# A fused gated linear attention and MLP kernel: first unit loaded and scanned in halves, three whole-weight tiles made split ones, a new order of the work, other idle fill-ups

## The chip, the cores and the metric

One core of a Trainium2 chip runs the kernel. Its engines are TensorE (PE, matrix products), VectorE (DVE), ScalarE (ACT), GpSimd (POOL) and SyncE (SP, which here only issues DMAs). The metric is the time of one execution on the chip in microseconds, the median of several runs.

## The reference

Gated linear attention over B=4 batches, H=8 heads, S=768 tokens and head size D=48, then an MLP on the heads put side by side (3072 tokens of 384 values, inner size 2048):

```python
f = 1.0 / (1.0 + np.exp(-f_logit))
for t in range(S):
    state = f[:, :, t, :, None] * state + np.einsum('bhd,bhe->bhde', k[:, :, t], v[:, :, t])
    y[:, :, t] = np.einsum('bhd,bhde->bhe', q[:, :, t], state)
x = y.transpose(0, 2, 1, 3).reshape(B * S, H * D)
h = x @ w_in                                   # 384 -> 2048
g = h * np.clip(h + 3.0, 0.0, 6.0) / 6.0
out = g @ w_out                                # 2048 -> 384
```

## The kernel before

**Units.** The attention goes in 24 units, each 128 tokens (a chunk, in two halves of 64) of one batch with all heads. A step of unit *i* is written `step.i`:

- `load`, `loadq`, `loadv`: DMAs of the gate logits, of q and k together, and of v, issued by SP.
- `gate` (L321, ACT): the sigmoid. `back` (L327, DVE): a scan backwards through the chunk, giving for each token the product of the gates behind it. `rend` (L343 and L344, DVE): the chunk's whole product, and one over it. `kmul` (L340, DVE or POOL): k times that scan. `fwd` (L347, DVE): the scan forwards. `qmul` (L353): q times it. `decay` (L356): the old state times the chunk's product.
- `tk` (L411, PE): transposes of k, copied out by `ktok` (L418, ACT). `kv` (L430, PE): the chunk's new state, added by `carry0` and `carry1`. `att` (L392, PE): scores of queries with keys, and `mask` (L399, DVE), which copies them out under the causal triangle. `qs` (L461) and `av` (L478, PE): queries with states, and scores with values, into one bank.
- `xh`, `xl`: the result x as two float16 parts, high and low. Where the order holds an `xs` (L501, PE), PE subtracts the high part in its bank and ACT writes `xl`; else DVE does. `hole`: a DMA that packs the rows.

**Weights.** They come as float64 bits in 16 tiles *f*: `ld` (DMA), then `z`, `cy`, `mid`, `dif`, `top` (integer operations on ACT and DVE that round the bits to float32: `whole`), then `high` and `low` (float16 parts: `weight`; `lowi` and `lowo` are the halves of `low` for `w_in` and `w_out`, in tiles 0 to 7).

**The MLP.** Tokens go in groups of up to 512, numbered so that the step of group *g* and tile *f* has index 16 *g* + *f*. `mm1` (L536): nine float16 products of 512 columns. `relu` (ACT), `g` (L550, DVE): the activation. `gh` (L555, ACT) and `gl` (L565, DVE or POOL): its float16 parts. `mm2` (L582): nine float16 products into three banks that stay open for the group. In the first group the tiles 0 to 4 are done in half groups, `mm1a`, `mm1b` (L603), `ga`, `gb` and `mm2a`, `mm2b` (L621), whose second products are float32 with `whole`. Its tiles 5, 6 and 7 have whole groups, but `mm2x` (L593): three float32 products of 512 columns with `whole`, without `gh` and `gl`.

**The order.** A table of words, `ORDER`, holds every step. The code walks it and emits each step's instructions, and a chain of dependencies then keeps each engine's instructions in just that order. The number behind a PE step is the PSUM bank. A table `ON_POOL` names the steps that go to GpSimd instead of DVE. So the order of the words sets what each queue waits for. Buffers are rings: gates and scans have three (unit 3 uses unit 0's), q/k and v four each.

**Idle products.** At the start the table holds words `warm.N`: float32 products of a zero tile `blank` into a bank that nobody reads, N times 128 columns:

```python
if op == "warm":
    for at in range(0, i, 4):
        n = min(i - at, 4)
        nc.tensor.matmul(
            idle[:, :n * 128].rearrange("p (a n) -> p a n", n=128), blank,
            blank.unsqueeze(1).broadcast_to([128, n, 128]), start=True, stop=True,
        )
```

Of the kernel before, what the change touches and what calls it, by code (L numbers as in the profile page):

```python
# [48 lines left out]
kmul.1 decay.4 kmul.6 lowi.5 kmul.7 decay.7 lowi.7 kmul.8 gl.9 decay.8 gl.11 qmul.8 gl.12 lowo.0 low.15 lowo.3 gl.19  # L49
decay.9 qmul.10 gl.25 kmul.12 gl.26 qmul.12 gl.27 gl.28 gl.29 gl.32 gl.33 decay.14 kmul.14 kmul.15 qmul.15 gl.37 gl.38  # L50
gl.39 gl.40 kmul.16 decay.15 gl.44 qmul.16 gl.45 gl.47 decay.17 kmul.18 gl.51 gl.52 gl.53 gl.54 gl.55 kmul.19 gl.57
decay.19 decay.20 kmul.20 qmul.20 kmul.21 gl.60 qmul.21 decay.22 gl.62 kmul.23 qmul.23 gl.70 gl.72 gl.74 gl.73 gl.75
gl.76 gl.77
# [3 lines left out]
carry0.0 load.2 qmul.0 warm.1 att.0.0 loadq.1 ld.0 rend.1 qs.0.2 mask.0 gate.2 warm.1 av.0 xh.0 kmul.1 tk.1.4 ktok.1  # L57
carry1.0 fwd.1 qmul.1 warm.3 att.1.0 xs.0 loadv.1 back.2 mask.1 rend.2 cy.0 load.3 kv.1.2 z.0 mid.0 loadq.2 gate.3
back.3 ld.1 carry0.1 warm.1 qs.1.0 dif.0 kmul.2 top.0 fwd.2 xl.0 carry1.1 loadq.3 av.1 hole.0 tk.2.4 rend.3 xh.1 xs.1
xl.1 z.1 qmul.2 warm.3 att.2.2 kmul.3 cy.1 mid.1 fwd.3 ktok.2 loadv.2 high.0 warm.4 kv.2.0 carry0.2 tk.3.4 ktok.3  # L60
mask.2 load.4 gate.4 qs.2.0 hole.1 av.2 xh.2 carry1.2 lowi.0 mm1a.0.4 relua.0 dif.1 qmul.3 top.1 high.1 ga.0 loadv.3
xs.2 att.3.2 mask.3 kv.3.0 ld.2 carry0.3 carry1.3 lowi.1 xl.2 loadq.4 warm.1 qs.3.2 av.3 xh.3 mm1a.1.4 cy.2 xs.3 xl.3
relua.1 z.2 back.4 kmul.4 rend.4 fwd.4 ga.1 decay.4 mm2a.0 qmul.4 load.5 gate.5 tk.4.1 mm2a.1 ktok.4 loadv.4 ld.3 cy.3
z.3 hole.2 mid.2 dif.2 top.2 att.4.2 kv.4.2 hole.3 mm1b.0.0 high.2 back.5 mid.3 relub.0 loadq.5 mm1b.1.1 relub.1
lowi.2 gb.0 dif.3 kmul.5 rend.5 gb.1 mm1a.2.4 mm1b.2.0 top.3 mm2b.0 mm2b.1 fwd.5 tk.5.1 relua.2 relub.2 gb.2 qmul.5
ld.4 z.4 cy.4 mid.4 mm2b.2 high.3 ktok.5 lowi.3 ga.2 mm1b.3.0 load.6 gate.6 loadq.6 dif.4 back.6 top.4 load.7 mm1a.3.4
ld.5 relub.3 mm2a.2 relua.3 ga.3 high.4 gb.3 cy.5 z.5 mask.4 mm2a.3 lowi.4 mm1a.4.1 relua.4 rend.6 ld.6 mm1b.4.4
relub.4 loadv.6 gate.7 loadq.7 mm2b.3 carry0.4 kmul.6 fwd.6 mid.5 ga.4 dif.5 z.6 qmul.6 top.5 cy.6 tk.6.1 ktok.6
mm2a.4 back.7 ld.7 decay.5 high.5 qs.4.2 decay.6 att.5.0 gb.4 av.4 kv.6.0 carry1.4 lowi.5 mm1.5.4 mask.5 mm2b.4
carry0.6 xh.4 z.7 xl.4 mid.6 dif.6 kmul.7 carry1.6 loadv.5 kv.5.2 ld.8 relu.5 g.5 mm2x.5 cy.7 top.6 high.6 cy.8 rend.7  # L70
tk.7.0 mid.7 dif.7 load.8 lowi.6 carry0.5 top.7 mm1.6.4 ktok.7 qs.5.2 fwd.7 qmul.7 high.7 loadv.7 relu.6 g.6 z.8
# [887 lines left out]
```

## Time and profile before

| | |
|---|---|
| time, three runs | 467.69, 466.12, 467.33 us, median 467.33 |
| the profiled execution | 468.3 us, its span 466.6 us, mean granted PE clock 0.993 |
| PE busy | 459.2 us (98%) |
| DVE busy | 300.1 us (64%) |
| ACT busy | 205.1 us (44%) |
| POOL busy | 79.3 us (17%) |
| DMA | 43.09 MB, mean 92 GB/s |

The span is what the profiler saw of the program; the execution's own time holds 1.7 us around it. Engines overlap, so the shares don't add up. Rows of a timeline hold a group of neighbouring instructions of one form: start, length in us, engine, line, operation, out<-in with shapes, and how many; a bracket holds the idle time ahead of it and what ended that. "xN" behind a PE row counts instructions as the profiler does: a float32 product is two of them, a float16 product one.

### The profile page before, as it was taken

The page shows a single profiled execution, that of the slowest core. Times are in us where ns is not written, and L with a number is a line of the kernel's source. Part 1 is how long each engine was busy: PE and PEld are TensorE (multiplying, and loading weights), DVE is VectorE, ACT ScalarE, POOL GpSimd, SP SyncE. Part 2 cuts the span into 40 slices and gives each one's busy share as a digit, 9 for nine tenths or more (in the row PEclk, how much of TensorE's full clock was granted, in tenths as well). Part 3 has the DMA queues.
Part 4 walks back from the last instruction along what each step waited for, and adds up shares of the span by engine and source line. Part 5 has one row for each costly group of instructions (what it writes and reads, how often), then busy time and mean ns, then how long its engine had stood idle before and what let it go on. Part 6 is the DMA issues. An engine that isn't in the chain of part 4 may idle for free.

```text
span 466.6 us, 11487 instructions
## 1 busy us (share of the span) xinstructions
PE 459.2 (98%) x4963; PEld 247.5 (53%) x4963; DVE 300.1 (64%) x508; ACT 205.1 (44%) x344; POOL 79.3 (17%) x85
## 2 busy tenths in 40 slices
...
PEclk9799999999999999999999999999999999999999
...
GB/s 301 188 249 353 249 181 249 198 84 0 135 108 1 51 206 0 153 46 0 87 31 91 42 94 1 196 90 76 4 80 0 1 0 6 24 45 3 0 1 68
DMA packets 25396, 43.09 MB, mean 92 GB/s; under 512 B 2560, under 2 KB 17152, under 8 KB 25344
## 3 DMA queue, kind: packets, MB, share of 16 engines
...
q8 instruction: 39, 0.64, 0.6%
...
## 4 chain that ended last, share of the span: by engine, by line
PE 97%; DVE 1%; ACT 1%; issue 1%; DVEq 0%
PE o L582 35%; PE pair L536 26%; PE single L536 13%; PE pair L461 3%; PE o L621 3%; PE pair L478 3%; PE pair L392 3%; PE pair L430 2%; PE idle L804 2%; PE o L593 2%; PE pair L636 1%; PE single L636 1%; PE single L603 1%; PE pair L603 1%; PE pair L411 1%; PE single L411 1%
## 5 line engine op out<-in xcount | busy, mean ns | idle before, releaser
L582 PE MATMUL o<-gg,weight 128*128 128x512 f16 x744 | 170.2, 379 | 0.0
L536 PEld LDWEIGHTS <-weight 128*128 128x128 f16 x819 | 78.7, 98 | 93.6 <-issue 0.8
L536 PE MATMUL pair<-xts,weight 128*128 128x512 f16 x549 | 125.9, 379 | 0.0
L582 PEld LDWEIGHTS <-weight 128*128 128x128 f16 x744 | 72.0, 98 | 82.4 <-issue 0.7
L555 ACT ACTIVATE gg<-tg 128x512 f16<-128x512 f32 x88 | 54.5, 627 | 62.5 <-DVE tg L550 56.1
L550 DVE SCALAR_TENSOR_TENSOR tg<-tg,pair 128x512 f32<-128x512 f32 x61 | 41.3, 682 | 62.7 <-ACT tg L546 62.6
L546 ACT ACTIVATE tg<-pair,half 128x512 f32<-128x512 f32 x61 | 41.5, 683 | 66.6 <-PE pair L536 64.8
L565 POOL TENSOR_TENSOR gg<-tg,gg 128x512 f16<-128x512 f32 x33 | 40.1, 1225 | 167.1 <-ACT gg L555 148.1
L536 PE MATMUL single<-xts,weight 128*128 128x512 f16 x270 | 63.3, 379 | 0.0
L550 DVE SCALAR_TENSOR_TENSOR tg<-tg,single 128x512 f32<-128x512 f32 x30 | 20.5, 683 | 33.2 <-ACT tg L546 33.2
L546 ACT ACTIVATE tg<-single,half 128x512 f32<-128x512 f32 x30 | 20.6, 686 | 45.0 <-PE single L536 43.3
L347 DVE TENSOR_TENSOR_SCAN suffix<-gates,rend 112x516 f32<-112x516 f32 x24 | 30.6, 1276 | 4.3 <-POOL qkf L340 3.7
L327 DVE TENSOR_TENSOR_SCAN suffix<-gates,unit 112x516 f32<-112x516 f32 x24 | 29.9, 1248 | 5.1 <-ACT gates L321 5.0
L565 DVE TENSOR_TENSOR gg<-tg,gg 128x512 f16<-128x512 f32 x39 | 27.0, 702 | 8.4 <-ACT gg L555 8.2
L497 ACT ACTIVATE xts<-pair 112x512 f16<-112x512 f32 x24 | 14.3, 595 | 30.2 <-PE pair L478 17.8
L340 POOL TENSOR_TENSOR qkf<-qkf,suffix 112x512 f32<-112x512 f32 x13 | 17.0, 1309 | 47.1 <-DVE suffix L327 43.4
L399 DVE TENSOR_TENSOR a<-pair,causal 128x512 f32<-128x512 f32 x24 | 16.4, 684 | 13.0 <-PE pair L392 10.2
L510 DVE SCALAR_TENSOR_TENSOR xts<-pair,xts 112x512 f16<-112x512 f32 x20 | 13.6, 682 | 8.5 <-ACT xts L497 8.4
L321 ACT ACTIVATE gates<-gates 112x512 f32<-112x512 f32 x24 | 14.9, 623 | 5.2 <-DMA gates<-fg 5.2
L430 PE MATMUL pair<-v,ktok 64*48 64x48 f32 (+1 forms) x768 | 15.8, 214 | 1.3 <-issue 1.3
L478 PE MATMUL pair<-a,v 64*48 64x64 f32 (+1 forms) x768 | 16.2, 222 | 0.6 <-DVE a L399 0.2
L392 PE MATMUL pair<-qkf 48*64 48x64 f32 x768 | 16.4, 224 | 0.2 <-ACT state L450 0.2
...
## 6 DMA issues: line engine op xcount, KB each, us to landing
...
xts<-xts SPq DMA_DIRECT2D x48, 24.0 KB, 1.9
...
```

The lines of the kernel that those rows point to most:

```text
L327: nc.vector.tensor_tensor_scan(flat(sf)[:, ::-1], gt[:, 1:][:, ::-1], flat(unit)[:, ::-1], 0.0, op0=ALU.mult, op1=ALU.add,)
L340: engine("kmul", i).tensor_tensor(parts_of(t, 1), parts_of(t, 1), split(sf[:, :, 1:C + 1]), op=ALU.mult)
L347: nc.vector.tensor_tensor_scan(flat(sf), gt[:, :NP * (C + 1)], flat(rend), 0.0, op0=ALU.mult, op1=ALU.add,)
L392: nc.tensor.matmul(d["at"][HC * odd:HC * (odd + 1), e, 2 * n + c], t[rs, 1, n, c, odd], t[rs, 0, n, c, odd], start=True, stop=True,)
L430: nc.tensor.matmul(d["kv"][r:r + m, odd, c, n], d["ktok"][rs, 2 * n + part, r:r + m], heads_of(vt[rs], part, n, e)[:, :D], start=(odd, e) ...
L478: nc.tensor.matmul(d["y"][to:to + m, odd, n, cs], heads_of(vt[rs], c, n, e)[:, :m], d["a"][rs, 2 * n + c, e], start=False, stop=True, skip ...
L536: nc.tensor.matmul(h, win[:, f, a, k * 128:(k + 1) * 128], g["xt"][:, k, :g["n"] // C, b], start=i == 0, stop=i == 3 * KT - 1,)
L546: nc.scalar.activation(d["t"], d["h"], AF.Relu, bias=half, scale=RISE)
L550: nc.vector.scalar_tensor_tensor(d["t"], d["t"], TOP, d["h"], op0=ALU.min, op1=ALU.mult)
L555: nc.scalar.activation(d["gg"][:, 0], d["t"], AF.Copy)
L565: engine("gl", int(g["name"]) * NF + f).tensor_tensor(d["gg"][:, 1], d["t"], d["gg"][:, 0], op=ALU.subtract)
L582: nc.tensor.matmul(g["o"][m], wout[:, f, a, m * 128:(m + 1) * 128], g[f]["gg"][:, b], start=f == 0 and i == 0, stop=f == NF - 1 and i == 2 ...
```

## The change

*The first unit.* Its gate logits come in two DMAs, `load.0` and `loadh.0`, and sigmoid and first scan are two each, `gate.0`, `gateh.0` and `back.0`, `backh.0`. k and q of this unit come apart, `loadk.0` ahead of `loadv.0` and `loadq.0`. All go by SP, as before.

*The start.* A dummy sigmoid that stood among the constants is now a word of the table (`table.0`), and one constant is set by DVE instead of POOL. A `brief.84` word makes 84 bfloat16 products of 64x64 columns on a zero tile; with `warm.8` behind them, two products of 512 columns, they stand where `warm.16`, four of them, stood. The other fill-ups ahead of the first model product were 4, 1, 1, 3, 1, 3 and 4 (x128 columns) and are 2, 7, 3, 1 and 3; the 1 behind it stays.

*Whole-weight tiles.* `mm2x` of tiles 5, 6 and 7 go; these tiles have `gh`, `gl` and the nine-product `mm2`, and their `lowo` stand earlier. `xs.4` and `xs.5` are new, so `xl.4` and `xl.5` go from DVE to ACT.

*The order and the engines.* The table is another one throughout. `ON_POOL` changes too: of the first group and the units beside it, `kmul.1`, `gl.9`, `gl.11`, `gl.12` and `lowo.3` go to DVE, and `lowi.0`, `lowi.6`, `decay.5`, `decay.6` and `gl.8` to GpSimd. Two output steps change their kind (`outv.4` to `outs.4`, `outs.6` to `outv.6`), and two output pieces of the fourth group are no longer written in halves.

```diff
-HALVED = [("3", 0), ("3", 1), ("4", 0), ("4", 1), ("4", 2)]
+HALVED = [("4", 0), ("4", 1), ("4", 2)]
 ...
 ORDER = """
-load.0 gate.0 back.0 loadq.0 loadv.0 rend.0 kmul.0 load.1 fwd.0 gate.1 back.1 warm.16 tk.0.3 ktok.0 warm.4 kv.0.0
 ...
+load.0 loadh.0 loadk.0 load.1 loadv.0 loadq.0 table.0 gate.0 loadq.1 gateh.0 gate.1 back.0 backh.0 kmul.0 brief.84 warm.8
+tk.0.2 rend.0 fwd.0 back.1 qmul.0 ktok.0 warm.2 kv.0.2 carry0.0 carry1.0 load.2 kmul.1 warm.7 tk.1.4 ktok.1 rend.1
 ...
+    small = const.tile([128, 128], BF16, name="small")
+    nc.vector.memset(small, 0.0)
     blank = const.tile([128, 128], F32, name="blank")
     nc.vector.memset(blank, 0.0)
     half = const.tile([128, 1], F32, name="half")
-    nc.gpsimd.memset(half, 2.0 ** (GBITS - HBITS - 1))
+    nc.vector.memset(half, 2.0 ** (GBITS - HBITS - 1))
     table = const.tile([128, 1], F32, name="table")
-    nc.scalar.activation(table, half, AF.Sigmoid)
 ...
+    def halved(sf, gt, rows):
+        fu = unit.rearrange("r p c -> r (p c)")
+        fs = sf.rearrange("r p c -> r (p c)")
+        n = NP // 2 * (C + 1)
+        cuts = 0, n + 1, FW
+        ops = {}
+        for p, name in enumerate(("", "h")):
+            lo, hi = cuts[p:p + 2]
+            at, two = slice(p * n, (p + 1) * n), slice(p * NP // 2, (p + 1) * NP // 2)
+            def load(_=None, lo=lo, hi=hi):
+                nc.sync.dma_start(out=gates[0][:, lo:hi], in_=fg[0][:, lo:hi])
+            def gate(_=None, two=two):
+                nc.scalar.activation(rows[:, two], rows[:, two], AF.Sigmoid)
+            def back(_=None, at=at):
+                nc.vector.tensor_tensor_scan(
+                    fs[:, at][:, ::-1], gt[:, 1:][:, at][:, ::-1], fu[:, at][:, ::-1], 0.0, op0=ALU.mult, op1=ALU.add,
+                )
+            ops.update({"load" + name: load, "gate" + name: gate, "back" + name: back})
+        def loadk():
+            t = sb.tile([128, 2, NP, C], F32, tag="qkf", name="qkf0")
+            nc.sync.dma_start(out=t[:, 1], in_=qk[0][:, 1])
 ...
+        def loadq():
+            nc.sync.dma_start(out=ops["tile"][:, 0], in_=qk[0][:, 0])
+        def first():
+            nc.scalar.activation(table, half, AF.Sigmoid)
 ...
+        if i == 0:
+            ops.update(halved(sf, gt, rows))
 ...
-        if op == "warm":
+        if op == "brief":
+            for _ in range(i):
+                nc.tensor.matmul(idle[:64, :64], small[:, :64], small[:, :64], start=True, stop=True)
+        elif op == "warm":
```

The order as the engines get it. TensorE from its first instruction to the first unit's `av`, before (`pair` and `single` are PSUM banks, `qkf` holds q and k, `a` the masked scores):

```order
L804 MATMUL idle<-blank 128x512 x4
L411 MATMUL pair_71<-ident,qkf_132 128x112 x4
L804 MATMUL idle<-blank 128x512
L430 MATMUL pair_70<-v_134,ktok_151 64x48
...
L804 MATMUL idle<-blank 128x128
L392 MATMUL pair_70<-qkf_132 64x64 x16
L461 MATMUL pair_71<-qkf_132,middle_101 64x64 x8
L804 MATMUL idle<-blank 128x128
L478 MATMUL pair_71<-a_212,v_134 64x64 x8
L478 MATMUL pair_71<-a_212,v_134 48x64 x8
L411 MATMUL single<-ident,qkf_198 128x112 x4
```

and in the changed kernel, where lines are shifted (L845 the small products, L849 the idle products, L453 `tk`, L472 `kv`, L434 `att`, L503 `qs`, L520 `av`):

```order
L845 LDWEIGHTS small
L845 MATMUL idle<-small 64x64
...
L849 MATMUL idle<-blank 128x512 x2
L453 MATMUL pair_71<-ident,qkf_132 128x112 x4
L849 MATMUL idle<-blank 128x256
L472 MATMUL pair_71<-v_135,ktok_242 64x48
...
L849 MATMUL idle<-blank 128x384
L453 MATMUL single<-ident,qkf_140 128x112 x4
L434 MATMUL pair_70<-qkf_132 64x64 x16
L503 MATMUL pair_71<-qkf_132,middle_102 64x64 x8
L849 MATMUL idle<-blank 128x384
L520 MATMUL pair_71<-a_300,v_135 64x64 x8
```

The second unit's `tk` (into `single`) has moved from behind the first unit's `av` to ahead of its `att`, and the small products, 168 instructions, stand at the head.

VectorE up to the mask of the third unit, `mask.2`. Before, from `mid.0` (L256) on:

```order
L256 TENSOR_SCALAR raw_200<-top_270 128x768
...
L343 TENSOR_SCALAR ends<-suffix_76 112x4
L344 RECIPROCAL rend<-ends 112x4
L353 TENSOR_TENSOR qkf_299<-qkf_299,suffix_80 112x512
L340 TENSOR_TENSOR qkf_321<-qkf_321,suffix_76 112x512
L256 TENSOR_SCALAR raw_303<-top_372 128x768
L347 SCALAR_TENSOR_TENSOR suffix_76<-gates_75,rend 112x516
L399 TENSOR_TENSOR a_413<-pair_71,causal 128x2x4x64
```

and in the changed kernel (L441 is the mask, L383 and L384 `rend`, L257 `mid`, L387 `fwd`):

```order
L367 SCALAR_TENSOR_TENSOR suffix_76<-gates_75,unit 112x516
L393 TENSOR_TENSOR qkf_417<-qkf_417,suffix_80 112x512
L380 TENSOR_TENSOR qkf_463<-qkf_463,suffix_76 112x512
L441 TENSOR_TENSOR a_499<-pair_71,causal 128x2x4x64
L383 TENSOR_SCALAR ends<-suffix_76 112x4
L384 RECIPROCAL rend<-ends 112x4
L257 TENSOR_SCALAR raw_495<-top_504 128x768
L387 SCALAR_TENSOR_TENSOR suffix_76<-gates_75,rend 112x516
```

`rend.3`, `mid.1` and `fwd.3` stood ahead of `mask.2` and now stand behind it. `kmul.1`, on GpSimd before, is now a step of DVE, the third behind `fwd.0`, and `back.0` is two scans of 258 columns.

More of the change, by code (lines that the diff above doesn't have):

```diff
@@ L48 @@
 ON_POOL = """
[L49 to L53, printed above, removed]
+lowi.0 decay.5 decay.4 kmul.6 decay.6 lowi.5 kmul.7 lowi.6 lowi.7 kmul.8 gl.8 decay.7 decay.8 qmul.8 low.15 gl.15
@@ L57 @@
[L57 to L71, printed above, removed]
@@ L72 @@
-decay.7 att.6.0 ld.9 lowi.7 gate.8 av.5 cy.9 z.9 mask.6 mm1.7.4 relu.7 mid.8 dif.8 top.8 mid.9 carry1.5 dif.9 high.8
-low.8 mm2x.6 mm1.8.0 g.7 loadq.8 ld.10 top.9 xh.5 cy.10 relu.8 high.9 back.8 rend.8 mm2x.7 ld.11 xl.5 g.8 att.7.2 z.10
-cy.11 qs.6.0 kv.7.2 mid.10 load.10 loadv.8 av.6 dif.10 low.9 top.10 z.11 mid.11 gh.8 mm1.9.4 ld.12 ld.14 xh.6 xl.6
-gl.8 mm2.8 dif.11 high.10 low.10 relu.9 g.9 cy.12 mm1.10.1 top.11 mask.7 kmul.8 carry0.7 gh.9 gl.9 hole.4 relu.10
-high.11 mm2.9 carry1.7 g.10 low.11 z.12 mid.12 ld.13 dif.12 top.12 cy.13 gh.10 gl.10 tk.8.1 ktok.8 mm1.11.0 z.13
@@ new lines @@
+tk.0.2 rend.0 fwd.0 back.1 qmul.0 ktok.0 warm.2 kv.0.2 carry0.0 carry1.0 load.2 kmul.1 warm.7 tk.1.4 ktok.1 rend.1
+fwd.1 att.0.0 mask.0 qs.0.2 warm.3 av.0 qmul.1 gate.2 back.2 att.1.0 mask.1 ld.0 z.0 load.3 xh.0 xs.0 cy.0 mid.0
+loadv.1 rend.2 dif.0 kv.1.2 carry0.1 carry1.1 warm.1 qs.1.0 av.1 xl.0 loadq.2 kmul.2 tk.2.4 gate.3 xh.1 ktok.2 top.0
+fwd.2 back.3 qmul.2 loadv.2 xs.1 kv.2.2 xl.1 high.0 carry0.2 loadq.3 warm.3 att.2.2 qs.2.0 kmul.3 tk.3.4 ld.1 z.1
+lowi.0 mask.2 load.4 hole.0 cy.1 rend.3 ktok.3 av.2 xh.2 gate.4 hole.1 mm1a.0.4 relua.0 xs.2 loadv.3 mid.1 fwd.3 dif.1
```

159 lines of the change are left out of this document (91 added, 68 removed).

## The prediction

> **What bounds the kernel now.** I read the page first, then a table of windows, then the first 30 us instruction by instruction.
>
> ```profile
> PE 459.2 (98%) x4963; PEld 247.5 (53%) x4963; DVE 300.1 (64%) x508; ACT 205.1 (44%) x344; POOL 79.3 (17%) x85
> PEclk9799999999999999999999999999999999999999
> q8 instruction: 39, 0.64, 0.6%
> PE 97%; DVE 1%; ACT 1%; issue 1%; DVEq 0%
> ```
>
> TensorE (PE) is busy for 98% of the span and carries 97% of the chain; its clock is below full speed only near the start. So time is won in two ways only: fewer columns for PE, or an earlier dense stage. Windows show who leads at the start (from 40 us on PE has no hole):
>
> ```profile
> 10.00:20.00 10.00, 8.17 (x222) 6.18 (x222) 9.66 (x15) 4.96 (x11) 0.45 (x1) 0.84 0.59 234
> 30.00:40.00 10.00, 9.87 (x169) 8.26 (x168) 9.83 (x18) 8.33 (x15) 0.51 (x1) 1.00 0.64 234
> 40.00:80.00 40.00, 40.00 (x553) 27.56 (x551) 37.49 (x71) 29.60 (x44) 6.44 (x6) 1.00 0.68 255
> 25.03:101.80 76.77, 76.46 (x1149) 50.85 (x1140) 68.78 (x122) 57.64 (x89) 12.99 (x13) 1.00 0.64 234
> 13.40:16.80 3.40, 1.93 (x74) 1.44 (x74) 3.33 (x7) 2.39 (x5) 0.00 (x0) 1.00 0.65 261
> 16.80:20.20 3.40, 3.31 (x66) 2.66 (x66) 3.40 (x6) 1.19 (x4) 0.00 (x0) 0.50 0.05 13
> 20.20:23.60 3.40, 3.40 (x40) 2.12 (x39) 1.37 (x4) 2.64 (x5) 0.00 (x0) 0.50 0.53 153
> ```
>
> After the window's length the columns are PE, weight loads, VectorE (DVE), ScalarE (ACT), GpSimd, then clock, DMA share and GB/s. DVE is full while the first units pass (9.66 of 10) and still 94% busy from 40 to 80 us, so it sets when PE can begin its dense stage, and may set its pace afterwards. The clock fell to half from 16.8 to 23.6 us.
>
> The DVE queue, by its timeline (start, duration):
>
> ```profile
> 4.13 1.23 DVE L327 TENSOR_TENSOR_SCAN suffix<-gates,unit 112x516 f32<-112x516 f32 x1 [2.32 <-ACT gates L321]
> 5.40 0.17 DVE L343 TENSOR_SCALAR ends<-suffix 112x4 f32<-112x4 f32 x1
> 5.77 0.66 DVE L340 TENSOR_TENSOR qkf<-qkf,suffix 112x512 f32<-112x512 f32 x1
> 6.46 1.23 DVE L347 TENSOR_TENSOR_SCAN suffix<-gates,rend 112x516 f32<-112x516 f32 x1
> 7.61 1.21 DVE L327 TENSOR_TENSOR_SCAN suffix<-gates,unit 112x516 f32<-112x516 f32 x1
> 10.89 0.69 DVE L399 TENSOR_TENSOR a<-pair,causal 128x512 f32<-128x512 f32 x1 [0.20 <-PE pair L392]
> 20.07 0.15 DVE L343 TENSOR_SCALAR ends<-suffix 112x4 f32<-112x4 f32 x1
> 20.34 0.66 DVE L353 TENSOR_TENSOR qkf<-qkf,suffix 112x512 f32<-112x512 f32 x1
> 23.61 0.36 DVE L256 TENSOR_SCALAR raw<-top 128x768 int16<-128x768 int16 x1 [2.00 <-ACT top L252]
> 23.89 1.23 DVE L347 TENSOR_TENSOR_SCAN suffix<-gates,rend 112x516 f32<-112x516 f32 x1
> 25.03 0.67 DVE L399 TENSOR_TENSOR a<-pair,causal 128x512 f32<-128x512 f32 x1
> 25.61 0.55 DVE L275 TENSOR_TENSOR weight<-whole,weight 128x384 f16<-128x384 f32 x1
> 26.08 0.55 DVE L263 TENSOR_TENSOR top<-top,raw 128x768 int16<-128x768 int16 x1
> 55.25 0.70 DVE L356 TENSOR_TENSOR decayed<-state,ends 112x192 f32<-112x192 f32 x2
> ```
>
> It starts at 4.13 and reaches `mask.2` (25.03), the last thing that PE needs before its first model product. In between it is idle 0.20 and 2.00 us, the latter because `mid.1` stands in the queue behind an ACT conversion. The PE timeline:
>
> ```profile
> 1.13 6.38 PE L804 MATMUL idle<-blank 128*128 128x512 f32 x8 [1.13 <-DVE blank L208]
> 7.34 0.55 PE L411 MATMUL pair<-ident,qkf 112*128 112x112 f32 x4
> 7.73 1.04 PE L804 MATMUL idle<-blank 128*128 128x512 f32 x2
> 8.70 0.91 PE L430 MATMUL pair<-v,ktok 64*64 64x48 f32 x48
> 9.53 0.49 PE L804 MATMUL idle<-blank 128*128 128x128 f32 x2
> 10.06 0.69 PE L392 MATMUL pair<-qkf 48*64 48x64 f32 x32
> 16.75 0.66 PE L430 MATMUL pair<-v,ktok 64*48 64x48 f32 x14 [1.27 <-issue]
> 27.33 1.16 PE L603 MATMUL single<-xts,weight 128*128 128x256 f16 x9
> 32.68 0.38 PE L501 MATMUL pair<-xts,less 112*112 112x256 f16 x2
> 32.90 1.46 PE L621 MATMUL o<-th,whole 128*128 128x256 f32 x6
> 61.00 2.84 PE L593 MATMUL o<-tg,whole 128*128 128x512 f32 x6
> 63.68 0.55 PE L411 MATMUL pair<-ident,qkf 112*128 112x112 f32 x4
> 80.73 2.11 PE L582 MATMUL o<-gg,weight 128*128 128x512 f16 x9
> 82.67 2.11 PE L536 MATMUL pair<-xts,weight 128*128 128x512 f16 x9
> ```
>
> **The sum, against the profiled execution** (468.3 us, span 466.6, 1.7 around it; the median of the runs is 467.33, 1.0 less).
>
> *Products, -1.8.* A whole-weight `mm2x` takes 63.68 - 61.00 = 2.68 us, a split `mm2` 82.67 - 80.73 = 1.94. Three are exchanged: 3 x 0.74 = -2.2. `xs.4` and `xs.5` are new, each 32.90 - 32.68 = 0.22: +0.4. PE is dense there, so all of it is on the path.
>
> *The start: when mask.2 begins.*
> - The first scan needs only half of load and sigmoid. Whole, the sigmoid ended 0.03 before the scan's 4.13. Both halves together cannot be quicker than one; what is won is that the second half's wait lies under the first half's scan. Bounds: 0 and half of a sigmoid plus half of a scan (0.6 + 0.6)/2 = 0.9 in all; I take -0.5, the middle.
> - The order puts `rend.3`, `mid.1`, `fwd.3` behind `mask.2`: by starts 0.27 + 0.28 + 1.14 = -1.7. It takes `kmul.1` from GpSimd: 6.46 - 5.77 = +0.7, and one more instruction of the scan, about +0.1. Net -0.9.
> - With `mid.1` gone from there, its wait goes, and the 0.20: -2.2. Bounds 0 (another wait takes its place) and 2.2.
> - What is late next is `mask.0`. The 84 products stream 64 columns once; a 512-column float32 product streams twice that of float16 (2.68/6 = 0.447 against 1.94/9 = 0.216), so one small one is a sixteenth: 0.028 at full clock, 0.056 at half; 84 at half are 4.7. From about 1.0 they end at 5.7. The two large ones are four instructions, 1.8 at full and 3.6 at half clock; I take 2.3, so `tk.0` at 8.0 (7.34 before). Then 0.39 + 0.97 to `kv.0` as now, 0.83, the new `warm.7` (2 x 0.447 + 2 x 0.335 = 1.6), `tk.1` 0.39, and 0.83 from `att.0` to `mask.0` (10.06 to 10.89): 13.0. DVE gets there at 3.63 + 1.3 (scan) + 0.7 + 0.4 + 1.15 + 1.13 + 0.6 + 0.7 + 0.4 + 1.15 = 11.2, plus about 0.3 for `kmul.1`, whose chunk came late to GpSimd too. So +1.5. Bounds 0 (full clock, -2.3) and 3.5.
> - PE's 1.27 without a releaser. It stands inside one group of products, so no operand can have been missing, and 39 packets of 16 KB on the instruction queue for 9926 PE instructions make one packet for 254 of them: I read it as PE waiting for its own instructions. The order shows 449 PE instructions ahead of it (a float32 product is four, a transpose two). In the changed kernel number 449 lies in the middle of `av.0`, ahead of `att.1`, since 168 small ones come first. There DVE has `qmul.1` and `back.2`, 1.8 us, as cover; without the cover `mask.1` waits. I take +1.1, bounds 0 (the packet has landed) and 2.2.
>
> Sum at `mask.2`: -0.5 - 0.9 - 2.2 + 1.5 + 1.1 = -1.0. From there to the first model product PE needed 27.33 - 25.03 = 2.30, since `kv.2` and `tk.3` stood behind; now they stand ahead, and only the mask (0.7) and `av.2` (0.62) remain: -1.0. The dense stage begins 2.0 earlier.
>
> [...]
>
> *Given back behind it, +1.5.* PE would now reach `att.8`, 102 us, 2.0 + 1.8 = 3.8 earlier. DVE begins that stretch 1.0 earlier, so has 76.8 - 2.8 = 74.0. Its work there was 68.78; it gains the three moved (1.7), four `gl` less two `xl` (2 x 0.70), three `lowo` less two `lowi` (0.47, 25.61 to 26.08), and loses two `decay` (0.70): 71.6, or 97%. Over 30 to 40 us it did 98%, over 40 to 80 94%; at 94% it would need 76.4, 2.4 late. Between 0 and 2.4 I take 1.5, nearer the long stretch.
>
> ```profile
> L565 DVE TENSOR_TENSOR gg<-tg,gg 128x512 f16<-128x512 f32 x39 | 27.0, 702 | 8.4 <-ACT gg L555 8.2
> ```
>
> At nothing: three `gh` and two `xl` more on ACT (29.60 of 40 busy). On SyncE (SP) the halves are two more issues ahead of `loadv.0`, which has 3 us to spare. `load.3` now stands ahead of `loadv.1` and holds it until `fwd.0` is done, near 7 us; `kv.1` wants it at 15. The tail's tokens are the same.
>
> Total: -2.0 - 1.8 + 1.5 = -2.3: 466.0 for a profiled execution, **465.0** against the median.
>
> **Rivals.**
> 1. *Neither loss comes* (the instructions have landed, DVE runs at 98%): -2.3 - 1.1 - 1.5 = -4.9, 462.4. For it: one exposed wait in 39 packets. Against: DVE had no 40 us that full.
> 2. *DVE becomes the bound from 30 to 102 us*, at the mean of its 90% (25 to 102) and 94%: 71.6/0.92 = 77.8, so 3.8 late instead of 1.5: 0.0, 467.3. Some of its idle time was only PE being behind, which speaks against.
> 3. *The clock rises one window later*, near 10 us: four large products at 3.6 instead of 2.3, `tk.0` and half of `kv.0` doubled, +2.0: 467.0.
> 4. *Slower: small products do not raise the clock*, and it stays half until 13.4. Then `kv.0`, `warm.7`, `tk.1` and `att.0` double as well, 3.3 more: -2.3 + 2.0 + 3.3 = +3.0, 470.3. It decides once the clock rises later than about 11 us. For it: from 16.8 to 20.2 PE showed 3.31 of 3.40 busy, nearly all small products, and the clock stayed half for another window. Against: those were gapped, the 84 are not. [...]
>
> **How the numbers follow.** Chances: forecast 0.42 (own range 463.8 to 466.4), rival 1 0.20, rival 2 0.16, rival 3 0.10, rival 4 0.12. About 0.3%, 1.4 us, is what can be told from no change. Faster: 0.42 + 0.20 = 0.62; same: 0.16 + 0.10 = 0.26; slower 0.12. The range leaves out rival 4 and the lower edge of rival 1: 462.0 to 468.6.
>
> **What would show it.** The first scan as two of about 0.6, the first near 3.6. The first transposes near 8 us, not before 6 or after 9. A hole on PE without a releaser inside `av.0`, about 13 us, and `mask.1` waiting for it. `mid.1` with no 2 us ahead of it. `mask.2` near 24.0, the first 128x256 product near 25.3. No L593 group, nine-product groups in its place. Between 40 and 100 us DVE at 95% or more, and PE with holes ahead of `mm2` groups where rival 2 holds. The clock row of the first 14 us decides rivals 3 and 4. The forecast is wrong if DVE still waits 2 us ahead of `mask.2`, or if holes in the later groups, where only the order changed, exceed 1 us.

## The result and the profile after

The changed kernel takes 473.81 us (median of 5 runs, 472.77 to 474.45), the kernel before 467.33: ratio 1.0147, interval 1.0124 to 1.017. It is slower by 6.5 us, where 2.3 less was forecast. The profiled execution took 474.3 us, its span is 472.4, 5.8 more than that of before. Two executions far outside the others in the experiments below (596 us at a mean clock of 0.75 in `a_ld1`, 484 us at 0.95 in `a_few_ld3`) are left out of the ratios.

From the page of the changed kernel, the lines that stood for before in the prediction:

```profile
span 472.4 us, 11681 instructions
PE 460.6 (98%) x5054; PEld 251.8 (53%) x5054; DVE 298.3 (63%) x508; ACT 206.9 (44%) x350; POOL 82.8 (18%) x88
PEclk9778999999999999999999999999999999999998
q8 instruction: 40, 0.66, 0.6%
PE 94%; DVE 3%; issue 1%; ACT 1%; DVEq 0%
```

PE still carries the chain, but "PE busy" hides the loss, since a product at half clock counts as busy (from 20.20 to 23.60 us, below, PE has 3.21 of 3.40 us busy at a clock of 0.50). The clock row has 7, 7 and 8 in its second to fourth slices, and the instruction queue one packet more. PE's timeline shows where:

```profile
1.06 4.49 PE L845 MATMUL idle<-small 128*64 128x64 bf16 x84 [1.06 <-DVE small L208]
7.30 0.55 PE L453 MATMUL pair<-ident,qkf 112*128 112x112 f32 x4
16.82 0.46 PE L520 MATMUL pair<-a,v 64*64 64x64 f32 x16
19.17 0.68 PE L520 MATMUL pair<-a,v 64*48 64x64 f32 x16 [1.89 <-issue]
27.09 1.16 PE L645 MATMUL single<-xts,weight 128*128 128x256 f16 x9
30.34 0.33 PE L503 MATMUL pair<-qkf,middle 48*64 48x64 f32 x3
32.71 0.70 PE L503 MATMUL pair<-qkf,middle 48*64 48x64 f32 x13 [2.04 <-issue]
62.38 2.12 PE L578 MATMUL single<-xts,weight 128*128 128x512 f16 x9
```

There are two holes without a releaser (the rows marked "issue"), one in the middle of `av.1` and one in the middle of `qs.3`. Before had one, in `kv.1`. From one instruction's start to the next the holes are 2.11 and 2.26 us, in before 1.49. The windows show what follows each of them (after the length: PE, PEld, DVE, ACT, POOL, clock, DMA share, GB/s):

```profile
13.40:16.80 3.40, 3.01 (x128) 2.34 (x120) 3.25 (x8) 2.59 (x7) 0.00 (x0) 1.00 1.04 413
16.80:20.20 3.40, 1.49 (x34) 1.23 (x35) 3.40 (x5) 0.91 (x3) 0.00 (x0) 0.80 0.29 103
20.20:23.60 3.40, 3.21 (x55) 2.36 (x54) 1.15 (x2) 2.66 (x6) 0.91 (x1) 0.50 0.05 12
30.60:34.00 3.40, 1.20 (x32) 0.97 (x32) 3.12 (x7) 0.44 (x1) 0.00 (x0) 0.77 0.75 275
34.00:37.40 3.40, 3.40 (x41) 2.68 (x34) 0.12 (x1) 1.23 (x3) 0.00 (x0) 0.50 0.04 11
62.38:466.66 404.28, 404.23 (x4077) 207.13 (x4072) 250.09 (x418) 169.29 (x285) 73.80 (x67) 1.00 0.21 66
```

VectorE's queue, in the changed kernel (first scan, `mask.0`, `mask.2`):

```profile
3.49 1.28 DVE L320 TENSOR_TENSOR_SCAN suffix<-gates,unit 112x258 f32<-112x258 f32 x2 [1.60 <-ACT gates L317]
12.18 0.69 DVE L441 TENSOR_TENSOR a<-pair,causal 128x512 f32<-128x512 f32 x1 [0.45 <-PE pair L434]
25.72 0.69 DVE L441 TENSOR_TENSOR a<-pair,causal 128x512 f32<-128x512 f32 x1 [4.37 <-PE pair L434]
```

It starts earlier than before and ends up waiting 4.37 us for PE. In the windows, one with a hole in it has PE busy 1.49 and 1.20 of 3.40, and the clock is at half in the next one. In the record each slow stretch is 6.83 us long; before had one, after has two. In the last row, from `mm1.5` to PE's last product, PE waits for nothing. For comparison that row of before, and from both timelines the last product and the last output DMA:

```profile
57.05:462.52 405.47, 405.38 (x4058) 207.09 (x4055) 250.98 (x420) 168.49 (x280) 71.74 (x65) 1.00 0.21 67
461.38 1.15 PE L636 MATMUL single<-gg,weight 128*128 128x256 f16 x9
462.97 0.38 ACTq L659 DMA_DIRECT2D outT<-os  x1
```

```profile
465.51 1.15 PE L678 MATMUL single<-gg,weight 128*128 128x256 f16 x9
467.11 0.38 ACTq L701 DMA_DIRECT2D outT<-os  x1
467.00:473.00 6.00, 0.00 (x0) 0.00 (x0) 0.00 (x0) 0.08 (x1) 0.00 (x0) 0.70 0.23 64
```

So the 5.8 us of span come in three pieces. `mm1.5` begins at 62.38 where it began at 57.05: +5.3. From there to the last product PE needs 404.28 where it needed 405.47: -1.2. From the last issue's end to the end of the span it is 466.6 - 463.35 = 3.2 before and 472.4 - 467.49 = 4.9 after: +1.7. In that tail the DMA record of after holds an instruction packet (16 KB, 467.39, 1.71 us long) among the output rows, and the last rows move at 470.2; before's last packet went at 452.3.

The +5.3 can be placed more closely. The first model product, `mm1a.0`, begins at 27.09 where it began at 27.33, so the loss lies behind it, on the way to `mm1.5`; first before, then after:

```profile
27.33:57.05 29.72, 29.59 (x489) 25.27 (x483) 27.69 (x51) 22.37 (x38) 3.34 (x4) 1.00 0.78 300
27.09:62.38 35.29, 33.05 (x483) 27.38 (x478) 29.62 (x53) 23.40 (x39) 5.37 (x6) 0.90 0.74 265
```

The stretch is 5.6 longer. PE is idle 2.2 of it, where it was idle 0.1, and busy 3.5 longer, at a mean clock of 0.90. The hole in `qs.3` and the slow clock behind it make up all of it.

**Where the holes are.** Counting PE's instructions (products, weight loads and the few others) in order of time, before's hole stands behind number 449, after's behind 705 and 1217: 449 + 256 and 449 + 4 x 256. The windows from 0 to the middle of each hole nearly show it, with 441, 697 and 1201 products and loads:

```profile
0.00:16.00 16.00, 13.88 (x220) 7.93 (x221) 12.13 (x24) 7.54 (x13) 4.23 (x17) 1.00 0.86 320
```

```profile
0.00:18.20 18.20, 15.62 (x348) 11.79 (x349) 14.13 (x31) 9.01 (x17) 2.72 (x15) 1.00 0.87 308
0.00:31.50 31.50, 26.89 (x600) 20.17 (x601) 23.01 (x45) 17.18 (x32) 3.63 (x16) 0.89 0.73 254
```

The instruction queue's packets fit to it. Around these holes each starts some time after PE enters the block before the one that it brings, 3.17 and 3.97 us for the two of after and 3.79 for that of before. For the block from 705 PE entered at 13.41, the packet moved at 16.58 and PE went on at 19.17; for that from 1217 these are 26.48, 30.45 and 32.71. PE had run through the 256 instructions between in 3.7 and 4.0 us.

### The profile page after: what moved, and what is told of

It is laid out like the page before. It is cut to its first block, busy times and chain, and to the rows that moved or that the text cites. A ratio compares the mean times of both kernels' runs of the same rounds, so it can differ in the third digit from the quotient of the medians.

```text
span 472.4 us, 11681 instructions
## 1 busy us (share of the span) xinstructions
PE 460.6 (98%) x5054; PEld 251.8 (53%) x5054; DVE 298.3 (63%) x508; ACT 206.9 (44%) x350; POOL 82.8 (18%) x88
## 4 chain that ended last, share of the span: by engine, by line
PE 94%; DVE 3%; issue 1%; ACT 1%; DVEq 0%
PE o L624 35%; PE pair L578 25%; PE single L578 13%; PE pair L503 3%; PE pair L520 3%; PE pair L472 3%; PE pair L434 2%; PE o L663 2%; PE idle L849 1%; PE pair L678 1%; PE single L678 1%; PE pair L453 1%; PE idle L845 1%; PE single L453 1%; PE pair L645 1%
## 5 line engine op out<-in xcount | busy, mean ns | idle before, releaser
L624 PE MATMUL o<-gg,weight 128*128 128x512 f16 x771 | 175.8, 379 | 0.0
L578 PEld LDWEIGHTS <-weight 128*128 128x128 f16 x819 | 78.5, 98 | 92.5 <-issue 0.8
L624 PEld LDWEIGHTS <-weight 128*128 128x128 f16 x771 | 74.7, 98 | 87.1 <-issue 0.7
L597 ACT ACTIVATE gg<-tg 128x512 f16<-128x512 f32 x91 | 56.4, 627 | 58.2 <-DVE tg L592 33.0
L607 DVE TENSOR_TENSOR gg<-tg,gg 128x512 f16<-128x512 f32 x41 | 30.1, 739 | 18.4 <-ACT gg L597 18.3
L387 DVE TENSOR_TENSOR_SCAN suffix<-gates,rend 112x516 f32<-112x516 f32 x24 | 29.8, 1241 | 0.7
L367 DVE TENSOR_TENSOR_SCAN suffix<-gates,unit 112x516 f32<-112x516 f32 x23 | 28.7, 1250 | 0.0
L441 DVE TENSOR_TENSOR a<-pair,causal 128x512 f32<-128x512 f32 x24 | 16.4, 684 | 14.6 <-PE pair L434 13.8
L552 DVE SCALAR_TENSOR_TENSOR xts<-pair,xts 112x512 f16<-112x512 f32 x18 | 12.4, 686 | 14.2 <-ACT xts L539 13.9
L380 POOL TENSOR_TENSOR qkf<-qkf,suffix 112x512 f32<-112x512 f32 x11 | 14.7, 1337 | 27.3 <-DVE suffix L367 23.9
L520 PE MATMUL pair<-a,v 64*48 64x64 f32 (+1 forms) x768 | 17.0, 224 | 2.2 <-issue 1.9
L602 DVE SCALAR_TENSOR_TENSOR gg<-tg,gg 128x512 f16<-128x512 f32 x16 | 11.0, 690 | 9.7 <-ACT gg L597 9.5
L434 PE MATMUL pair<-qkf 48*64 48x64 f32 x768 | 16.8, 224 | 0.0
L268 DVE SCALAR_TENSOR_TENSOR whole<-top,whole 128x768 int16<-128x768 int16 x16 | 16.4, 1022 | 0.2
```

The lines of the kernel that those rows point to most:

```text
L268: nc.vector.scalar_tensor_tensor(upper, conv[f]["y"], 8.0, upper, op0=ALU.mult, op1=ALU.add)
L367: nc.vector.tensor_tensor_scan(flat(sf)[:, ::-1], gt[:, 1:][:, ::-1], flat(unit)[:, ::-1], 0.0, op0=ALU.mult, op1=ALU.add,)
L387: nc.vector.tensor_tensor_scan(flat(sf), gt[:, :NP * (C + 1)], flat(rend), 0.0, op0=ALU.mult, op1=ALU.add,)
L434: nc.tensor.matmul(d["at"][HC * odd:HC * (odd + 1), e, 2 * n + c], t[rs, 1, n, c, odd], t[rs, 0, n, c, odd], start=True, stop=True,)
L441: nc.vector.tensor_tensor(d["a"].rearrange("r p e t -> r e p t"), d["at"], causal.unsqueeze(1).unsqueeze(1).broadcast_to([128, 2, NP, HC]) ...
L520: nc.tensor.matmul(d["y"][to:to + m, odd, n, cs], heads_of(vt[rs], c, n, e)[:, :m], d["a"][rs, 2 * n + c, e], start=False, stop=True, skip ...
```

## The experiments

Two things are edited: words of the order, and the loop that emits the idle products. Theory F is the block fetch above: that a packet is asked for when the block before is entered, and waits behind data, is how the author reads those packet times. Its rivals, named in the expectations, are P (a hole belongs to the work that PE does at that place), C (small products cost by themselves), K (a fetch takes a fixed time) and W (a weight tile comes too late). Times are medians, with the ratio to before and its interval behind them; profiles are of one execution each. `a_` kernels start from the changed one, `b_` kernels from the one before. A median of 466.4 to 466.6 was measured for before beside them. A slow stretch of the clock does not follow each hole in each run: before itself has runs at a mean clock of 0.993 (467.87 to 468.86) and at 0.996 or more (466.03 to 468.08), with medians of 468.0 to 468.4 and 466.2 to 466.5 in the four sets beside these experiments, so one stretch costs it about 2 us, and its profiled execution was one with a stretch.

**1. Large idle products again** (`a_undo`).

```diff
-... kmul.0 brief.84 warm.8
+... kmul.0 warm.16
```

> The changed kernel with four large idle products (16 instructions) where 84 small and two large ones (176) stood; all else as changed. Theory F (fetch): PE's holes without a releaser come where its instruction number is 449 + 256 k, because a block of 256 instructions is fetched only when the block before it is entered, and the packet waits behind data. With 160 fewer instructions ahead, number 449 falls into kv.1, 705 into att.2 and 961 into kv.3: a hole near kv.1, none in av.1 or in qs.3; one hole and its slow clock less (2.3 + 3.4) and the last fetch no longer among the output rows (1.6): 473.8 - 7.3 = 466.5, between 465 and 468.5. Theory P (place): the holes belong to what PE does in av.1 and qs.3 (operands, banks). Then they stay there, and the time is 473 to 474.5.

469.5 us, ratio to before 1.0066 (1.0043 to 1.0089), single runs 466.93 to 471.69.

```profile
17.88 0.43 PE L472 MATMUL pair<-v,ktok 64*48 64x48 f32 x13 [2.08 <-issue]
0.00:17.00 17.00, 14.16 (x221) 8.10 (x221) 12.79 (x29) 7.28 (x13) 2.72 (x15) 1.00 0.87 316
```

The hole went to `kv.1`, behind number 449, and there is none in `av.1` or `qs.3`: theory P falls. 4.3 us came back, not 7.3: this one hole is 2.3 long, and seven of the eight runs have a clock of 0.993 or less. The profiled execution is the eighth, the fastest, without a slow stretch; so no profile shows where the other runs lost their time.

**2. Sixteen instructions fewer** (`a_76`).

```diff
-... brief.84 warm.8
+... brief.76 warm.8
```

> The changed kernel with 76 small products for 84, that is 16 PE instructions fewer. Theory F: both holes stay, 16 instructions later in the program (still av.1 and near qs.3's end), but instruction 10177, which opens the last block, is no longer reached, so that no packet of 16 KB moves among the last output rows: the time from the last product to the end of the span falls from 5.7 to about 4.1, and the total by 1.6, to 472.2 (471.7 to 472.8). Theory P, or a tail that is slower for another reason (order of output steps): nothing moves, 473.3 to 474.3, the tail stays 5.7.

472.82 us, 1.012 (1.0087 to 1.0154).

```profile
20.67 0.33 PE L520 MATMUL pair<-a,v 64*48 64x64 f32 x8 [2.46 <-issue]
33.31 0.33 PE L503 MATMUL pair<-qkf,middle 48*64 48x64 f32 x5 [2.06 <-issue]
```

Where 16 and 13 products of a group were left behind the holes, 8 and 5 are left now: both moved by 8 products and their 8 loads. A short one (0.72) is new at number 449. The tail is a miss: it stayed at 4.9 us, with a packet at 465.59, though number 10177 lies 9 behind the last instruction. Why that packet still moved is not shown.

**3. The same time in fewer instructions** (`a_few`).

```diff
-            for _ in range(i):
-                nc.tensor.matmul(idle[:64, :64], small[:, :64], small[:, :64], start=True, stop=True)
+            for _ in range(i):
+                nc.tensor.matmul(
+                    idle[:64].rearrange("p (a n) -> p a n", n=128), small[:, :64],
+                    small.unsqueeze(1).broadcast_to([128, 4, 128]), start=True, stop=True,
+                )
-... brief.84 warm.8
+... brief.11 warm.8
```

> The changed kernel with 11 bfloat16 products of 512 columns (22 instructions) in the place of the 84 of 64 columns (168), about as long. Theory F: as with four large products, number 449 falls into kv.1 (14 instructions earlier in the program), one hole, no late fetch: 466.5, 465 to 468.5. Rival C (clock): that the products are small and many, not that they are many instructions, cost the time; also then about 467, but the holes without a releaser would stay in av.1 and qs.3. Theory P: 473 to 474.5.

465.85 us (464.21 to 468.05, 11 runs), 0.998 (0.9964 to 0.9997): 8 us faster than the changed kernel, as expected. Against before it is 0.2%, less than the 0.3% that the prediction would tell from no change.

```profile
1.06 4.58 PE L845 MATMUL idle<-small 128*64 128x512 bf16 x11 [1.06 <-DVE small L208]
7.40 0.55 PE L453 MATMUL pair<-ident,qkf 112*128 112x112 f32 x4
16.60 0.55 PE L472 MATMUL pair<-v,ktok 64*64 64x48 f32 x20 [0.98 <-issue]
```

11 products take 4.58 us where 84 took 4.49, and the first transposes begin at 7.40 where they began at 7.30. So the clock and the time of the small products are not what cost; their number of instructions is. The hole is behind number 449 and 1.2 us long, and the tail is 3.2.

**4. The small products in the old order** (`b_brief`).

```diff
-... back.1 warm.16 tk.0.3
+... back.1 brief.84 warm.8 tk.0.3
```

> The kernel before with only the small products: 84 of them and two large idle ones in the place of four large ones, 160 PE instructions more at the head. Theory F: number 449 falls into av.0 of the old order, 705 into tk.2 or its neighbours' end (av.1), 961 into mm1a.0's stretch behind kv.2, 1217 into kv.3's neighbours; the hole that stood in kv.1 is gone, one to three others come at those numbers, and the time is 467 to 473. Theory P: the hole stays in kv.1 and the time is that of before, 466.5 to 468.

473.35 us, 1.0149 (1.0126 to 1.0172), just above the expected range: this one edit makes the kernel before as slow as the changed one.

```profile
12.70 0.32 PE L480 MATMUL pair<-a,v 64*48 64x64 f32 x5 [0.61 <-issue]
308.47 0.43 PE L432 MATMUL pair<-v,ktok 64*64 64x48 f32 x12 [0.61 <-issue]
```

The hole in `kv.1` is gone, and one stands in `av.0`, where number 449 now lies. It is short (0.83), that at 705 shorter (0.29). A third one, of 0.83 again, stands far behind the start, at number 7617, which is 449 + 28 x 256. The record has 10.2 us of half clock, and in the tail a packet at 467.16, with 4.3 us from the last issue to the end. What brought the slow clock was not taken apart.

**5. A weight DMA later** (`a_ld1`), **and a second one** (`a_ld13`).

```diff
-... kmul.3 tk.3.4 ld.1 z.1 lowi.0 mask.2 load.4 hole.0 cy.1 ...
+... kmul.3 tk.3.4 lowi.0 mask.2 load.4 hole.0 ld.1 z.1 cy.1 ...
 (and in a_ld13)
-... tk.4.4 ld.3 xl.3 hole.2 ga.1 ...
+... tk.4.4 xl.3 hole.2 ld.3 ga.1 ...
```

> The changed kernel, but the DMA of weight tile 1 (768 KB, issued at 9.5 us) stands behind hole.0 in SP's order, so that it starts near 17 us. The PE program is the same. Theory F with queueing: the fetch of the block from 705 is asked for at 13.4 and moved at 16.6, just when the data issued up to 9.96 us have drained; with 768 KB less ahead it moves near 14.9 and is ready near 17.2: the hole in av.1 falls from 2.1 to under 0.8, that in qs.3 stays at 2.0 to 2.4; time 470.5 (468.5 to 472). Theory K (fetch latency is fixed, data do not matter): both holes as they were, 473 to 474.5. Rival W (the weight tile becomes late): mid.1 and mm1a.1 wait for it, a new wait of PE on an operand near 33 us, and 474 or more.

> As the run before, and the DMA of weight tile 3 (768 KB, issued near 25.5) behind hole.2, near 31. Theory F: the fetch of the block from 1217, asked for at 26.5 and moved at 30.5, moves 1.5 to 2 us earlier; the hole in qs.3 falls from 2.26 to under 0.8, too; both stretches of slow clock are gone in most runs: 467.5 (466 to 470), of which 1.6 are still the late fetch in the tail. Theory K: 473 to 474.5. Rival W: waits of PE for tile 3 before mm1b.3, near 45 us.

470.69 us, 1.0085 (1.0056 to 1.0114), as expected, and 470.73, 1.0096 (1.007 to 1.0122), a miss: the second DMA brought nothing more. The first has no profile that can be compared. In the second no hole without a releaser is left: the packet for 705 moved 1.19 us after the block before was entered (3.17 in the changed kernel), that for 1217 2.16 (3.97). But a wait is new:

```profile
26.05 1.35 PE L645 MATMUL single<-xts,weight 128*128 128x256 f16 x9 [2.36 <-ACT ktok L460]
```

`z.1` stands in ACT's queue ahead of `ktok.3` and waits 3.2 us for the tile that comes later; `mm1a.0` needs the bank that `ktok.3` empties. So with two DMAs of 768 KB put off the two packets came early enough, with the same PE instructions: theory K (a fixed latency) falls. The time that it gave went into the new wait and the tail, which stayed at 4.9.

**6. Both at once** (`a_few_ld`), and three tries to free what waited (`a_few_ld2`, `a_ld2`, `a_few_ld3`).

```diff
 (a_few_ld: 3 and both moves of 5; a_few_ld2, and a_ld2 with the 84 small products)
-... hole.0 ld.1 z.1 cy.1 rend.3 ktok.3 av.2 xh.2 gate.4 hole.1 mm1a.0.4 ... mid.1 fwd.3 dif.1 ...
+... hole.0 ld.1 rend.3 ktok.3 av.2 xh.2 gate.4 hole.1 z.1 cy.1 mm1a.0.4 ... fwd.3 ... qmul.3 mid.1 dif.1 ...
-... hole.2 ld.3 ga.1 ... loadv.4 dif.2
+... hole.2 ga.1 ... loadv.4 ld.3 dif.2
 (a_few_ld3: as a_few, but)
+... hole.1 ld.1 mm1a.0.4 ... fwd.3 ... qmul.3 z.1 cy.1 mid.1 dif.1 ...
```

> Both DMAs moved, and 11 products of 512 bfloat16 columns in place of the 84 small ones. Theory F: the hole at instruction 449 (kv.1) was 1.2 there; it stays between 0 and 1.2, and slow clock in few runs; the scatter between runs shrinks: 465.0 (464 to 466). Theory K: as without the moved DMAs, 465.9 with single runs up to 468.

> 11 products of 512 columns in place of the 84 small ones, both weight DMAs late as before, and what waited for tile 1 set behind what does not: z.1 and cy.1 on ACT behind ktok.3, mid.1 on DVE behind fwd.3 and qmul.3, ld.3 behind loadv.4. Theory F: no hole without a releaser over 0.5 us in the first 50 us, and the 2.2 us that PE waited for ktok.3 ahead of mm1a.0 are gone: 468.8 to 469.3 less 2.2 to 3: 466, and with full clock throughout 464.5 (464 to 467). Rival W: PE waits for tile 1 at mm1a.1 instead: 468 to 469.5.

> The same order of the two DMAs and of z.1, cy.1 and mid.1, with the 84 small products of the changed kernel left in. Theory F: 84 small products cost only through the place of the block boundaries and the fetch behind data; with data out of the way both holes stay gone, as they were in the run with both DMAs late, and ktok.3 does not wait: 470.7 less 2.4 = 468 (467 to 469.5), 1.6 of it the late fetch in the tail. Theory K: 473.

> 11 products of 512 columns in place of the 84; the DMA of weight tile 1 behind hole.1 (near 21 us), z.1, cy.1 and mid.1 behind qmul.3. Theory F: the fetch of the block from 449 finds 768 KB less ahead of it: a hole of at most 0.6 in kv.1 (1.2 before), and mm1a.0 waits neither for ktok.3 nor for the rows of hole.1: mm1a.0 near 23.5 where it was 26.5, full clock in most runs. If tile 1 is then ready in time: 464.0 (463 to 465.5). Rival W: mm1a.1 waits for tile 1 (landed near 25, converted by 31 to 32), which takes all of it back: 465.5 to 467.

469.25 us (1.0056, 1.0036 to 1.0076), 468.38 (1.0028, 1.0007 to 1.0048), 471.89 (1.0095, 1.0061 to 1.0129) and 469.15 (1.0043, 1.0024 to 1.0061): all misses, all slower than `a_few`. The first has no hole but 2.23 of waiting for `ktok.3`. In the second, which has a short hole (0.62) in `kv.1`, `mm1a.0` waits for the rows of `hole.1`, which move behind the 768 KB:

```profile
24.37 2.08 PE L645 MATMUL single<-xts,weight 128*128 128x256 f16 x9 [1.59 <-DMA xts<-xts]
```

In the third the fetch of one block came late again: PE entered the block before 961 at 18.09, the packet moved at 22.53, 4.4 later, with the DMA engines at 0.58 of their share between. That it met the moved data is the author's estimate. The holes are back:

```profile
18.09 0.44 PE L520 MATMUL pair<-a,v 64*48 64x64 f32 x16 [0.78 <-issue]
24.90 0.68 PE L520 MATMUL pair<-a,v 64*64 64x64 f32 x30 [1.62 <-issue]
31.19 0.69 PE L503 MATMUL pair<-qkf,middle 48*64 48x64 f32 x13 [0.88 <-issue]
```

The fourth had a hole of 2.0 in `kv.1` although the DMA was not ahead of it. The queueing of that one tile does not explain it; the DMA engines had 1.04 of their share from entering the block to the packet, with other data. Each of the four has a wait of one kind or the other; whether the start can be had without any stays open.

**7. More instructions, yet faster** (`a_116`).

```diff
-... brief.84 warm.8
+... brief.116 warm.4
```

> The changed kernel with 116 small products and one large in the place of 84 and two: 60 PE instructions more, about as long. Theory F: both holes stay, 60 instructions earlier in the program (in qs.1 and in att.3). At the end instruction 10177 is passed 67 instructions before the last product, so its packet moves before the output rows and none among them: the time from the last product's start to the end of the span falls from 6.0 to about 4.3, the total from 473.8 to 472.2 (471.5 to 473). Rival: the tail's 1.6 comes from the order of output steps: no change, 473.3 to 474.5.

468.85 us, 1.0037 (1.0018 to 1.0057), 5 us less than the changed kernel with 60 PE instructions more.

```profile
span 469.0 us, 11741 instructions
18.75 0.70 PE L503 MATMUL pair<-qkf,middle 48*64 48x64 f32 x14 [2.09 <-issue]
465.37 0.38 ACTq L701 DMA_DIRECT2D outT<-os  x1
```

The tail is 469.0 - 465.75 = 3.2 again, with no packet in it (the last went at 455.67). The hole behind 705 moved 60 instructions, into `qs.1`, and is 2.30 long. The one at 1217 is gone, against the expectation: that fetch came 2.00 after its block was entered, and not 3.97. Of the 5.0 us between the medians the tail is 1.7; the rest is not taken apart. The profiled execution (470.97 us) has 13.65 us of half clock behind its one hole, as much as the changed kernel has behind two.

**8. The products, taken back alone and made alone** (`a_few_mm2x`, `b_split`).

```diff
 (a_few_mm2x, from a_few, for k = 5, 6, 7; b_split is the reverse on before, with lowo.k and gl.k on GpSimd)
-... gh.k ... gl.k ... mm2.k ...
+... mm2x.k ...
```

> The kernel with 11 products of 512 columns, but tiles 5, 6 and 7 of the first group again with three float32 products (mm2x), without gh and gl. The prediction's term: 3 x 0.74 = 2.2 more on PE, and DVE has two gl of 0.70 and more less, so up to 1.5 given back: +0.7 to +2.2 against 465.85, I expect +1.5, 467.3. If DVE were the bound there, 0.

> The kernel before, with only the products changed: mm2 with gh and gl for tiles 5, 6 and 7 in the place of mm2x, the three lowo ahead of them and the three gl on GpSimd, nothing else. The prediction's term alone: -3 x 0.74 = -2.2 if nothing is given back, -0.7 if 1.5 are given back to a DVE that is full, 0 if PE waits for gl from GpSimd instead. In the changed order restoring mm2x cost 1.91 from mm1.5 on, so I expect -1.9: 464.6 (463.8 to 465.8). The start of the program, its one hole in kv.1 and its tail stay as they are.

469.23 us (467.3 expected), 1.0042 (1.0022 to 1.0062), and 470.81 (464.6 expected), 1.0075 (1.0051 to 1.0099). Taking the split tiles out of `a_few` costs 3.4 us in the medians; in the profile, from `mm1.5` to PE's last product, the one row of it against the 404.28 above (and 404.26 in `a_few`):

```profile
55.89:462.06 406.17, 406.12 (x4068) 207.87 (x4063) 248.46 (x415) 167.52 (x282) 72.91 (x67) 1.00 0.21 66
```

1.9 us, and PE waits for nothing there with them or without. The 1.9 lies in the expected range (0.7 to 2.2). The rest of the 3.4 is not explained: the two profiled executions took 468.11 us and, with a slow stretch that the first has not, 468.05. Put into the old order the split tiles lose 4, a miss: from `mm1.5` to PE's last product it takes 409.72 where before took 405.47. Between 55 and 90 us PE waits for the weights, and once for DVE's `xl`, as the longest rows of its table of waits say.

```profile
PE single L536 <- ACT weight L272: 1.3, 1, 1.3
PE single L536 <- POOL weight L275: 1.3, 1, 1.3
PE pair L392 <- DVE xts L510: 1.2, 1, 1.2
```

In ACT's queue a `gh` that waits for DVE stands ahead of `high.6`, and on GpSimd `gl.6` stands ahead of `lowi.7`, which `mm1.7` waits for. Of the two orders only the new one, whose words convert these weights earlier, has room for the split tiles.

**9. The first unit whole** (`a_few_whole`).

```diff
-load.0 loadh.0 loadk.0 load.1 loadv.0 loadq.0 table.0 gate.0 loadq.1 gateh.0 gate.1 back.0 backh.0 kmul.0
+load.0 load.1 loadq.0 loadv.0 table.0 gate.0 loadq.1 gate.1 back.0 kmul.0
```

> The kernel with 11 products of 512 columns, but unit 0 loaded, put through the sigmoid and scanned whole (q and k in one DMA ahead of v). The prediction's term: the first scan begins 0.6 later, 0 to 0.9 at mask.2; from there half of it at most reaches the end, because PE waits behind its own products: +0.5 (0 to 0.9), 466.3. It also moves when data and fetches meet, so up to one window of slow clock (2 to 3) in single runs.

469.85 us, 1.0062 (1.0039 to 1.0085): 4.0 more than with halves, not 0.5.

```profile
4.17 1.23 DVE L367 TENSOR_TENSOR_SCAN suffix<-gates,unit 112x516 f32<-112x516 f32 x1 [2.28 <-ACT gates L361]
6.65 0.69 DVE L380 TENSOR_TENSOR qkf<-qkf,suffix 112x512 f32<-112x512 f32 x1 [1.25 <-DMA qkf<-qk]
```

and in `a_few`:

```profile
3.44 1.28 DVE L320 TENSOR_TENSOR_SCAN suffix<-gates,unit 112x258 f32<-112x258 f32 x2 [1.55 <-ACT gates L317]
4.76 0.69 DVE L380 TENSOR_TENSOR qkf<-qkf,suffix 112x512 f32<-112x512 f32 x1
```

Against `a_few` the scan begins 0.73 later, and `kmul.0` 1.89 later, since k now comes with q. The hole in `kv.1` is 1.6. But `mm1.5` begins only 0.16 later, and the two profiled executions, with one slow stretch of 6.83 each, are only 0.4 apart (468.47 and 468.05). Two of the eleven runs have a clock of 0.996 or more (467.57 and 468.46), seven of `a_few`'s. So more frequent slow stretches are a part of the 4.0; what the rest is, no profile shows.

## Why the prediction was wrong

*The instruction fetch is the main step that failed.* The prediction read the wait without a releaser rightly as PE's own instructions and took the block's size from the packets. But it followed number 449 alone. It had the numbers for the next ones, and did not ask how fast PE runs through 256 instructions there: 3.7 us at `av.1` and 4.0 at `qs.3`, against 5.8 and 6.2 from entering a block to going on. At 449 itself, where it put +1.1, there was no hole. It also said that `mask.1` would be the loser; the hole in `av.1` held up the whole of unit 2, and `mask.2` came at 25.72 after a wait of 4.37 on DVE, not at 24.0.

*The clock after a hole had no price.* The window that fell to half in before stood in the prediction as a row, but as a fact of the start, not as what a hole costs. 6.8 us more at half clock are up to 3.4 us more of work, and the holes are 2.11 + 2.26 - 1.49 = 2.9 more: 6.3 together, against 5.3 at `mm1.5`. By this sum `mm1.5` would have been at most about 1 us earlier without them, not 2.0. The rival "small products do not raise the clock" came nearest in time (470.3) for a reason that was wrong: the clock record is full from 5.15 to 18.81, and `tk.0` began at 7.30, not at the forecast 8.0.

*The start's largest gain, -2.2, was not there to be had.* The prediction put DVE's 2.00 ahead of `mid.1` down to its place behind an ACT conversion. `b_split` has the same start as before, and its profiled execution has full clock there:

```profile
21.96 0.36 DVE L256 TENSOR_SCALAR raw<-top 128x768 int16<-128x768 int16 x1 [0.57 <-ACT top L252]
```

So 1.4 of the 2.0 came with PE's slow clock: ACT had waited 1.55 and 0.76 us for PE ahead of that conversion, and in `b_split` 0.65 and 0.52. In the new order the wait is at `mask.2` and for PE: 4.37 in the changed kernel, 3.23 in `a_few`, 1.33 in `a_undo` at full clock. Profiles with full clock up to `mm1a.0` compare the two starts: the old one (`b_split`) reaches it at 25.16 with a hole of 1.46, the new one at 25.91 with 2.29 (`a_undo`) and at 24.04 with 0.92 (`a_few_mm2x`). With each hole taken off in full that is 23.7 against 23.6 and 23.1, a gain of 0.1 to 0.6; the forecast, without the 1.1 for a hole, had 3.1. What sets PE's pace there in the new order was not taken apart.

*The tail was costed at nothing*, because its steps are the same. It took 4.9 us with a packet of instructions among the last rows, 1.7 more than before; in experiment 7, without that packet, it took 3.2.

*The products were sized well, the give-back was not there.* Three `mm2x` are worth 1.9 of the 2.2; with the two `xs` and the rest of the order the stretch is 1.2 shorter, against 1.8. The +1.5 for a DVE that is too full between 30 and 102 us did not come: from `mm1.5` on PE waits for nothing in before, after or `a_few`. A DVE busy for 94 to 95% from 40 to 80 us (37.77 of 40 in the changed kernel, 38.17 in `a_few`) is one that works ahead here, not a bound. What was costed at nothing, "three `gh` more on ACT", is one of the waits by which the same tiles lose 4 us in the old order.

*The halves were right in kind.* Two scans of 258 columns, the first at 3.49, were forecast (3.6). `kmul.0` gains more, 1.89, from the line without a price, k ahead of q; the two were not taken apart, and what they are worth at the end stays open (0.4 in the profiles, 4.0 in the medians).

*The late first unit was put too high.* `mask.0` was forecast at 13.0, with DVE waiting 1.5 for it. It came at 12.18 and DVE waited 0.45, with the clock full from 5.15 us on. `mid.1` has no 2 us ahead of it any more, as said, but for another reason than was given.

Behind 38 of the 39 packets before and 38 of the 40 after there is no hole. The three with one are early: PE ran through the 256 instructions ahead of the hole in 4.7, 3.7 and 4.0 us, and the DMA engines had 1.03, 1.03 and 0.95 of their share from entering the block to the packet.
